# First feed-forward layer, second pass: six blocks of 512 tokens in place of eight of 384

## The chip, the cores and the metric

The kernel runs on one core of a Trainium2 chip. The metric is the device time of one execution in microseconds, median of several runs. The kernel before takes 2503.87 us (three runs, 2503.05 to 2504.59).

## What is computed

Three stages follow one another; `N` is 3072 tokens, the model width is 512.

```python
x = attention(q, k, v, mem_k, mem_v)        # chunks of 32 queries, 16 + 32 + 8 keys and 8 memory keys, 8 heads
h = x @ w_in                                # [3072, 512] @ [512, 2048]
g = h * np.clip(h + 3.0, 0.0, 6.0) / 6.0
x = g @ w_out                               # [2048, 512]: the "first layer" ends here
logits = x @ w_gate                         # 8 experts
P = exp(logits - logits.max())
for _ in range(8):                          # rows and columns in turn
    P /= P.sum(1, keepdims=True) + 1e-9
    P /= P.sum(0, keepdims=True) + 1e-9
    P *= N / 8
out = sum(P[:, e:e+1] * (np.maximum(x @ w1[e], 0) @ w2[e]) for e in range(8))
```

## The kernel before

Every large product is made of three matmuls in the float32r type: operands are split into a high and a low part, and `passes` (L224 to L228) issues high x high, high x low and low x high into the same accumulator. In the trace these are the lines L226, L227 and L228.

The first layer's inner width of 2048 is taken in two halves of 1024, the two **passes** `pe` = 0 and 1, each over all tokens in eight blocks `b` of `B1` = 384 tokens and, inside a block, over eight slices `f` of 128 inner columns. The list `steps` holds all (pe, b, f); the main loop near the end of the function walks it with the index `i`, 64 steps to a pass. A step of pass 1 issues

- `first(i)`: `layer_product` (12 matmuls into `ph`: four slices of the model width, three matmuls each), `layer_relu` on ACT (L399, tile `t`) and `layer_times` on DVE (L404);
- `first_parts(i)`: `layer_high` (L166 on DVE in pass 1, tile `hh`) and `layer_low` (L421 on DVE, tile `hl`);
- `second(i - LAG)` with `LAG` = 2: 12 matmuls into the four accumulators `pa` with the `hh` and `hl` of two steps earlier. At a block's last slice it calls `evacuate`: four DVE adds (L503) of `pa` to the `x2` of pass 0, which `x2_load` fetched from DRAM (`xp`, L483); the sums go back to DRAM as `x2d` in `spill` (L445).

Beside this, each block of pass 1 carries: `x_load(b + 1)` at f = 1 (the attention's result from DRAM, L509, tile `xl`, stored in units of `UQ` = 96 tokens), `x_split` at f = 3 to 6, one slice of the model width each (ACT L210 for `xh`, DVE L215 for `xl`), `x2_load(b)` at f = 4, and the gates of finished blocks: `gate_logits` (L524, four small matmuls per block, each shown as two rows), `gate_copy` (ACT, L529) and `gate_turn` (three transposes L537 and a DVE reduction L538). Gates are made at f = 3, two blocks together in blocks 2, 4 and 6 and one in block 7, the last one after the loop.

Two further jobs run under pass 1. `factory` makes 80 sums of the experts' weights: SP loads 512 KB (L640), POOL adds (L645), SP stores (L648); a table of start times in units of steps paces them. From step (1, 4, 0) `x_ops` prepares the first 1024 tokens for the experts, one piece per step: loads from `x2d` (L710, three buffers `xb`), DVE subtractions (L719), and splits into `xo` (L210 on ACT, L215 on DVE). In the last block the experts' first weights are loaded (`w1_load`, L787 and others) and copied and split (`w1_hi` on ACT, L806; `w1_lo` on DVE, L811), a piece per step from f = 1 on.

The order of instructions on each engine is the order in which the program issues them; DMAs are issued by SP, in order. The matmuls of the experts' stage that follows are 512 or 256 tokens wide.

Of the kernel before, what the change touches and what calls it, by code (L numbers as in the profile page):

```python
# [9 lines left out]
F32 = mybir.dt.float32  # L10
F32R = mybir.dt.float32r
# [9 lines left out]
UQ = 96  # L21
# [43 lines left out]
def attn_moe_moe(ctx: ExitStack, tc: tile.TileContext, qk, vw, wi, wo, wa, wb, wg, out):  # L65
# [5 lines left out]
    NTT = NT // 128  # L71
    NB1, NSB = NT // B1, NT // (2 * HB)
    UPB = B1 // UQ
# [25 lines left out]
    half = const.tile([128, 1], F32, name="half")  # L99
    wgs = const.tile([128, KT + 1, 32], F32, name="wgs")  # L100
    Pm = const.tile([128, NTT, NE], F32, name="Pm")
# [3 lines left out]
    xd = [dr_p.tile([128, B1 // UQ, KT, UQ], F32, name=f"xd{b}") for b in range(NB1)]  # L105
    xp = [dr_p.tile([128, KT, B1], F32, name=f"xp{b}") for b in range(NB1)]
    ws1 = [dr_p.tile([128, 4, 2, 256], F32, name=f"ws1{j}") for j in range(NP // 2)]
# [279 lines left out]
    g_t, acc_t, x2_t = {}, {}, {}  # L387

    def layer_product(i):
        pe, b, f = steps[i]  # L390
        wh, wl = (w.rearrange("p (k f) -> p k f", k=KT) for w in wts["a", pe, f])
        g_t[i] = ps = ps_h.tile([128, B1], F32, tag="h", name="ph")
        for kt in range(KT):
            hi, lo = (t[:, kt] for t in xs[pe, b])
            passes(ps, wh[:, kt], wl[:, kt], hi, lo, kt == 0, kt == KT - 1)

    def layer_relu(i):
        t = h_p.tile([128, B1], F32, tag="t", name="t", bufs=2)
        nc.scalar.activation(out=t, in_=g_t[i], func=AF.Relu, scale=1.0 / 6.0, bias=half)  # L399
        g_t[i] = g_t[i], t  # L400
# [11 lines left out]
    def layer_high(i, eng=nc.scalar):  # L412
        t = g_t[i]
        hh = h_p.tile([128, B1], F32R, tag="hh", name="hh")
        copy(hh, t, nc.vector if steps[i][0] else eng)
        g_t[i] = t, hh

    def layer_low(i):
        t, hh = g_t[i]
        hl = h_p.tile([128, B1], F32R, tag="hl", name="hl")  # L420
        nc.vector.tensor_tensor(out=hl, in0=t, in1=hh.bitcast(F32), op=ALU.subtract)  # L421
        g_t[i] = hh, hl
# [5 lines left out]
    def second(i, out=True):  # L428
        pe, b, f = steps[i]
        turns = (0, NF // 2) if (pe, b) in ((0, 0), (0, 1)) else (0,)  # L430
        new, last = f in turns, f + 1 in turns or f == NF - 1
        if new:
            acc_t[pe, b] = [ps_a.tile([128, 512], F32, tag="a", name="pa")[:, :B1] for _ in range(4)]
# [47 lines left out]
    def x2_load(b):  # L481
        t = x2_t[b] = x2_p.tile([128, KT, B1], F32, tag="x2", name="x2")
        nc.sync.dma_start(out=t, in_=xp[b])  # L483

    def evacuate(pe, b, f):
        acc = acc_t.pop((pe, b))
        if pe == 0 and b in x2_t:
            x2 = x2_t.pop(b)
            for t in range(4):
                nc.vector.tensor_tensor(out=x2[:, t], in0=x2[:, t], in1=acc[t], op=ALU.add)  # L490
            spills.append((xp[b], x2))
        elif pe == 0:
            x2 = x2_p.tile([128, KT, B1], F32, tag="x2", name="x2")
            for t in range(4):
                nc.scalar.activation(out=x2[:, t], in_=acc[t], func=AF.Copy)
            if f < NF - 1:
                x2_t[b] = x2
            else:
                spills.append((xp[b], x2))
        else:  # L500
            x2 = x2_t[b]
            for t in range(4):
                nc.vector.tensor_tensor(out=x2[:, t], in0=x2[:, t], in1=acc[t], op=ALU.add)  # L503
            spills.append((x2d[:, :, b * B1:(b + 1) * B1], x2))
            later.append(b)

    def x_load(b):
        t = xf_t[b] = xl_p.tile([128, UPB, KT, UQ], F32, tag="xl", name="xl")
        nc.sync.dma_start(out=t, in_=xd[b])  # L509

    def x_split(b, kt):
        if kt == 0:
            xs[1, b] = x_tiles()
        hi, lo = (t[:, kt].rearrange("p (u q) -> p u q", u=UPB) for t in xs[1, b])
        split(hi, lo, xf_t[b][:, :, kt])

# [4 lines left out]
    def gate_logits(b):  # L521
        ps = ps_s.tile([128, B1], F32, tag="s", name="lg")
        for kt in range(KT):
            nc.tensor.matmul(ps[32 * kt:32 * kt + 32], wgs[:, kt], x2_t[b][:, kt], start=True, stop=True)  # L524
        lg[b] = ps

    def gate_copy(b):
        ps, lg[b] = lg[b], sm_p.tile([128, B1], F32, tag="lt", name="lt", bufs=1)
        nc.scalar.activation(out=lg[b], in_=ps, func=AF.Copy)  # L529

    def gate_turn(b):
        if b < NB1 - 1:
            ps = ps_s.tile([128, B1 // 128, 128], F32, tag="s", name="lg")
        else:
            ps = bank().rearrange("p (t k) -> p t k", k=128)[:, :B1 // 128]
        for i in range(B1 // 128):
            nc.tensor.transpose(ps[:, i], lg[b][:, 128 * i:128 * i + 128], ident)  # L537
        nc.vector.tensor_reduce(  # L538
            out=Pm[:, 3 * b:3 * b + 3], in_=ps.rearrange("p t (k e) -> p t e k", k=KT)[:, :, :NE],
            axis=AX.X, op=ALU.add)  # L540

    def sinkhorn():
# [13 lines left out]
        for _ in range(8):  # L556
            rs = sm_p.tile([128, NTT], F32, tag="rs", name="rs")
            nc.vector.tensor_reduce(out=rs, in_=Pm, axis=AX.X, op=ALU.add)
# [125 lines left out]

    def x_quarters(form, r0, r1, eng=nc.vector):

        l, h = slice(0, 256), slice(256, 512)
        quarter_tile(form)
        quarter_parts(form, ("B11",), r0[:, l])
# [13 lines left out]
    def x_ops(sb, p, tag):  # L703
# [3 lines left out]
        def load(n, kt, half_):  # L707
            xq[n] = p.tile([128, 2, HB], F32, tag=tag, name="xb", bufs=3)
# [6 lines left out]
        for n in X_ORDER:  # L715
# [11 lines left out]
            yield  # L727
        yield from x_quarters("B21", xq["B21"][:, 0], xq["B21"][:, 1])

# [351 lines left out]
    with tc.manual_schedule():  # L1081
# [17 lines left out]
        starts = [15 + 1.27 * j for j in range(len(jobs))]  # L1099
        xb_ctx = ctx.enter_context(ExitStack())  # L1100
        for i, (pe, b, f) in enumerate(steps):
            if i < 2 * NF:
# [9 lines left out]
            if (pe, b, f) == (1, NB1 - 1, 0):  # L1112
                assert build is None and begun[2] == len(jobs)
# [13 lines left out]
            for stage_, late in ((2, 2.6), (0, 0), (1, 1.3)):  # L1127
                while begun[stage_] < len(jobs) and starts[begun[stage_]] + late <= i:
                    jobs[begun[stage_]][stage_]()
                    begun[stage_] += 1  # L1130
# [4 lines left out]
            if pe == 1 and f == 1 and b + 1 < NB1:  # L1135
# [5 lines left out]
            if ready and f == 4:  # L1141
                gate_copy(later[0])
            first(i)
            if pe or due:
                first_parts(i)
            if due:
# [30 lines left out]
            r = f - 3  # L1177
            if 0 <= r < KT and n < NB1 and (pe or b == NB1 - 1):
# [231 lines left out]
```

## Time and profile before

| | |
|---|---|
| runs, median (lowest to highest) | 2503.87 us (2503.05 to 2504.59) |
| the profiled execution's own time | 2502.63 us |
| its span | 2500.8 us |
| PE busy | 2488.2 us, 99% of the span |
| DVE busy | 1971.4 us, 79% |
| ACT busy | 1444.4 us, 58% |
| POOL busy | 955.4 us, 38% |
| TensorE clock granted | 9 tenths or more in each of 40 slices |
| DMA | 586.72 MB, mean 235 GB/s |

The span goes from the first to the last instruction of the profiled execution; its own time is 1.8 us more. Starts of matmuls are recorded, their ends are modelled, so the spacing of matmuls is read from their starts. Pass 1 of the first layer lies between 378 and 657 us of the span.

### The profile page before, as it was taken

What the parts mean: (1) busy time and instruction counts of PE and PEld (TensorE: products, weight loads), DVE (VectorE), ACT (ScalarE), POOL (GpSimd) and SP (SyncE); (2) the same over time, 40 slices, a digit from 0 to 9 for tenths busy, and PEclk for the clock granted to TensorE, in tenths of its full rate; (3) what the DMA queues carried; (4) which work ended last, traced back from release to release, by engine and by line L of the source; (5) the groups of instructions that cost most, each with busy time, mean ns of one, the idle gap of its engine ahead of it and who ended that gap; (6) DMA issues with size and microseconds to landing.
All of it is one profiled execution on the core that took longest, in us unless ns stands there. A gap on an engine that the chain in (4) does not pass through costs nothing. (4 is left out here: it accounts for less than half of the span.)

```text
span 2500.8 us, 37810 instructions
## 1 busy us (share of the span) xinstructions
PE 2488.2 (99%) x13525; PEld 2172.8 (87%) x13525; DVE 1971.4 (79%) x2432; ACT 1444.4 (58%) x2647; POOL 955.4 (38%) x705
## 2 busy tenths in 40 slices
PE   9999999999999999999999999999999999999999
PEld 8999999999878888888888888888888888888888
DVE  8767656576689999999996778777887678777777
ACT  8666652222365555556666656556666666655665
POOL 0155656564026453544443324333333233232331
PEclk9999999999999999999999999999999999999999
DMA  7689979877466667766667777666777666676664
GB/s 209 190 277 310 305 267 312 268 272 244 129 210 207 225 208 233 232 228 218 233 223 264 266 249 247 223 217 231 251 266 233 226 221 231 225 235 208 215 220 157
DMA packets 373754, 586.72 MB, mean 235 GB/s; under 512 B 30324, under 2 KB 227133, under 8 KB 373565
## 3 DMA queue, kind: packets, MB, share of 16 engines
q1 hardware_dynamic: 373280, 584.06, 71.7%
q8 instruction: 106, 1.74, 0.3%
q14 instruction: 84, 0.68, 0.1%
q10 hardware_dynamic: 284, 0.24, 0.0%
HBM read 443.57 MB, written 140.61 MB: 234 GB/s over the span
## 5 line engine op out<-in xcount | busy, mean ns | idle before, releaser
L933 POOL TENSOR_TENSOR g<-g,pb 128x512 f32<-128x512 f32 x304 | 578.4, 1920 | 1175.6 <-ACT g L926 830.4
L984 ACT ACTIVATE oh<-g 128x1024 fp32r<-128x1024 f32 x336 | 355.1, 1057 | 356.9 <-PE oa L228 107.1
L989 DVE TENSOR_TENSOR ol<-g,oh 128x1024 fp32r<-128x1024 f32 x336 | 458.5, 1366 | 54.0 <-ACT oh L984 53.8
L645 POOL TENSOR_TENSOR fr<-fr 128x256 f32<-128x256 f32 x320 | 268.6, 840 | 191.4 <-DMA fr<-in_wa_dram 109.2
L226 PE MATMUL ga<-xo,w1h 128*128 128x512 f32 (+1 forms) x864 | 313.8, 363 | 1.4 <-ACT g L901 0.8
L228 PE MATMUL ga<-xo,w1l 128*128 128x512 f32 (+1 forms) x864 | 312.2, 361 | 0.0
L227 PE MATMUL ga<-xo,w1h 128*128 128x512 f32 (+1 forms) x864 | 312.2, 361 | 0.0
L959 DVE TENSOR_TENSOR g<-g 128x1024 f32<-128x1024 f32 x192 | 306.0, 1632 | 0.0
L227 PE MATMUL oa<-ol,w2h 128*128 128x512 f32 x760 | 297.9, 392 | 0.4 <-DVE ol L989 0.4
L226 PE MATMUL oa<-oh,w2h 128*128 128x512 f32 x760 | 297.3, 391 | 0.0
L228 PE MATMUL oa<-oh,w2l 128*128 128x512 f32 x760 | 295.7, 389 | 0.0
L806 ACT ACTIVATE w1h<-w1s 128x512 fp32r<-128x512 f32 (+1 forms) x416 | 249.7, 600 | 35.3 <-issue 16.0
L399 ACT ACTIVATE t<-ph,half 128x384 f32<-128x384 f32 x128 | 74.8, 584 | 242.2 <-PE ph L228 235.9
L918 DVE TENSOR_TENSOR g<-g,ga 128x512 f32<-128x512 f32 x192 | 130.5, 680 | 103.4 <-PE ga L228 103.4
L926 ACT ACTIVATE g<-g 128x512 f32<-128x512 f32 x288 | 178.2, 619 | 53.4 <-DVE g L918 53.1
L226 PE MATMUL gc<-xo,w1h 128*128 128x512 f32 (+1 forms) x544 | 195.4, 359 | 2.3 <-ACT g L901 1.8
L228 PE MATMUL gc<-xo,w1l 128*128 128x512 f32 (+1 forms) x544 | 194.5, 357 | 0.0
L227 PE MATMUL gc<-xo,w1h 128*128 128x512 f32 (+1 forms) x544 | 194.4, 357 | 0.0
L843 ACT ACTIVATE w2h<-w2s 128x1024 fp32r<-128x1024 f32 x168 | 176.8, 1052 | 27.5 <-DMA w2s<-in_wb_dram 21.7
L226 PEld LDWEIGHTS ga<-xo,w1h 128*128 128x128 f32 x864 | 162.5, 188 | 34.6 <-ACT g L901 2.4
L227 PEld LDWEIGHTS ga<-xo,w1h 128*128 128x128 f32 x864 | 162.5, 188 | 28.6
L228 PEld LDWEIGHTS ga<-xo,w1l 128*128 128x128 f32 x864 | 162.4, 188 | 25.2
(184 smaller groups left out, 5779.1 us busy)
## 6 DMA issues: line engine op xcount, KB each, us to landing
w1l<-wl SPq DMA_DIRECT2D x232, 256.0 KB, 4.2
w2l<-wl SPq DMA_DIRECT2D x112, 512.0 KB, 3.7
w1s<-ws SPq DMA_DIRECT2D x192, 256.0 KB, 4.9
w2s<-ws SPq DMA_DIRECT2D x96, 512.0 KB, 5.0
ws<-fr SPq DMA_DIRECT2D x80, 512.0 KB, 5.0
w2s<-in_wb_dram SPq DMA_DIRECT2D x144, 256.0 KB, 3.6
wl<-w1l SPq DMA_DIRECT2D x128, 256.0 KB, 4.2
wl<-w2l SPq DMA_DIRECT2D x56, 512.0 KB, 4.2
```

Of the source, the lines that this page charges most:

```text
L226: nc.tensor.matmul(ps, wh, xh, start=start, stop=False, skip_group_check=more)
L227: nc.tensor.matmul(ps, wh, xl, start=False, stop=False, skip_group_check=more)
L228: nc.tensor.matmul(ps, wl, xh, start=False, stop=stop, skip_group_check=more)
L645: nc.gpsimd.tensor_tensor(out=o, in0=a, in1=b, op=f)
L806: nc.scalar.activation(out=w1_part(g, w1[g]), in_=w1_part(g, w1s[g]), func=AF.Copy)
L843: nc.scalar.activation(out=hi, in_=w2s[m], func=AF.Copy)
L918: nc.vector.tensor_tensor(out=g, in0=g, in1=ps, op=ALU.add)
L926: nc.scalar.activation(out=g, in_=g, func=AF.Relu)
L933: nc.gpsimd.tensor_tensor(out=g, in0=g, in1=p, op=ALU.mult)
L959: nc.vector.tensor_tensor(out=o, in0=gq[n, x, i], in1=gq[n, y, i], op=ALU.subtract)
L984: nc.scalar.activation(out=hi, in_=gq[n, b, i], func=AF.Copy)
L989: nc.vector.tensor_tensor(out=lo, in0=gq[n, b, i], in1=op[m, i].bitcast(F32), op=ALU.subtract)
```

## The change

Pass 1 (the second pass) takes tokens in `NB2` = 6 blocks of `B2` = 512, so it has 48 steps instead of 64; pass 0 keeps its 64 steps of 384. What goes with it:

- The split x of pass 1 no longer takes a new pair of tiles per block. Three pairs of the old tiles are taken once and seen as pieces [128, 3, 512]: even blocks use pair 0 and one piece of pair 1, odd blocks pair 2 and another piece of pair 1. The third piece of pair 1 holds two units of 96 tokens of the x that is loaded, since the one `xl` tile holds four units and a block touches up to six.
- A block of 512 does not begin on a unit of 96, so `x_load` issues three or four transfers, and `x_split` makes three or four pieces per slice of the model width.
- `x2` of a block fills both buffers of its pool, half of the model width in each: two loads, two spills. The pass-0 result lies in one DRAM tensor `xpd`.
- The gates of each block are made at f = 3 of the next, all in one step, 512 tokens at a time (four transposes).
- The paced jobs count a step of pass 1 as `PACE` = 1.308 steps and are also looked at half-way through a step.
- `x_ops` starts at step (1, 2, 6), with two `xb` buffers; a third piece lies in the `xo` tile that is filled last. The experts' first weights begin two slices later in the last block (f = 2 for the loads, f = 3 to 6 for the copies).

```diff
-    steps = [(pe, b, f) for pe in range(2) for b in range(NB1) for f in range(NF)]
+    steps = [(pe, b, f) for pe in range(2) for b in range((NB1, NB2)[pe]) for f in range(NF)]
...
         for kt in range(KT):
-            hi, lo = (t[:, kt] for t in xs[pe, b])
+            hi, lo = (t[:, kt] for t in xs[pe, b]) if pe == 0 else xs[pe, b][kt]
             passes(ps, wh[:, kt], wl[:, kt], hi, lo, kt == 0, kt == KT - 1)
...
     def x2_load(b):
-        t = x2_t[b] = x2_p.tile([128, KT, B1], F32, tag="x2", name="x2")
-        nc.sync.dma_start(out=t, in_=xp[b])
+        x2_t[b] = []
+        for j in range(2):
+            t = x2_p.tile([128, KT, B1], F32, tag="x2", name="x2").rearrange("p k n -> p (k n)")
+            t = t[:, :2 * B2].rearrange("p (k n) -> p k n", k=2)
+            nc.sync.dma_start(out=t, in_=xpd[:, 2 * j:2 * j + 2, b * B2:(b + 1) * B2])
+            x2_t[b].append(t)
...
     def x_load(b):
-        t = xf_t[b] = xl_p.tile([128, UPB, KT, UQ], F32, tag="xl", name="xl")
-        nc.sync.dma_start(out=t, in_=xd[b])
+        if b < 2:
+            xq.extend(x_pieces() for _ in range(2 - b))
+        for kt in range(KT):
+            n, at = ((0, kt) if kt < 3 else (1, 0)) if b % 2 == 0 else ((2, kt) if kt < 3 else (1, 1))
+            xs.setdefault((1, b), []).append([t[:, at] for t in xq[n]])
+        u = b * B2 // UQ
+        t = xl_p.tile([128, UPB, KT, UQ], F32, tag="xl", name="xl")
+        spare = [v[:, 2, :KT * UQ].bitcast(F32).rearrange("p (k q) -> p k q", k=KT) for v in xq[1]]
+        c = UPB - u % UPB
+        nc.sync.dma_start(out=t[:, :c], in_=xd[u // UPB][:, UPB - c:])
+        if c < UPB:
+            nc.sync.dma_start(out=t[:, c:], in_=xd[u // UPB + 1][:, :UPB - c])
+        for i in range(2):
+            v = u + UPB + i
+            nc.sync.dma_start(out=spare[i], in_=xd[v // UPB][:, v % UPB])
...
     def gate_turn(b):
-        if b < NB1 - 1:
-            ps = ps_s.tile([128, B1 // 128, 128], F32, tag="s", name="lg")
+        if b < NB2 - 1:
+            ps = ps_s.tile([128, B2 // 128, 128], F32, tag="s", name="lg")
...
+        def sums_due(i):
+            now = i if i <= NB1 * NF else NB1 * NF + (i - NB1 * NF) * PACE
+            for stage_, late in ((2, 2.6), (0, 0), (1, 1.3)):
+                while begun[stage_] < len(jobs) and starts[begun[stage_]] + late <= now:
+                    jobs[begun[stage_]][stage_]()
+                    begun[stage_] += 1
...
-            if (pe, b) == (1, NB1 - 1) and 1 <= f <= AHEAD:
-                w1_hi(f - 1)
-                w1_lo(f - 1)
-                if f < AHEAD:
-                    w1_load(f + 3)
+            if (pe, b) == (1, NB2 - 1) and 3 <= f <= AHEAD + 2:
+                w1_hi(f - 3)
+                w1_lo(f - 3)
+                if f < AHEAD + 2:
+                    w1_load(f + 1)
...
-            if pe == 1 and f == 4:
+            if pe == 1 and f == 5:
                 x2_load(b)
-            ready = pe == 1 and (f == 3 and len(later) > (b < NB1 - 1) or f == 4 and later and later[0] in lg)
+            ready = pe == 1 and f == 3 and later
...
-            if (pe, b, f) == (1, 4, 0):
+            if (pe, b, f) == (1, 2, 6):
                 build = x_ops(0, xb_p, "xb")
```

Where instructions move, engine by engine. On DVE in the last block of the first pass, where the first x of the second pass is split (`wal`, `wbl`: low parts of the layer's weights; `xl`: low part of x), before:

```order
L404 SCALAR_TENSOR_TENSOR t<-t,ph 128x384
L421 TENSOR_TENSOR hl<-t,hh 128x384
L215 TENSOR_TENSOR wal<-sa,wah 128x512
L215 TENSOR_TENSOR wbl<-sb,wbh 128x512
L215 TENSOR_TENSOR xl<-xl,xh 128x384
```

and with the change:

```order
L410 SCALAR_TENSOR_TENSOR t<-t,ph 128x384
L427 TENSOR_TENSOR hl<-t,hh 128x384
L218 TENSOR_TENSOR wal<-sa,wah 128x512
L218 TENSOR_TENSOR wbl<-sb,wbh 128x512
L218 TENSOR_TENSOR xl<-xl,xh 128x384
L218 TENSOR_TENSOR xl<-xh 128x96
L218 TENSOR_TENSOR xl<-xl,xh 128x32
```

The split of one slice has become three pieces (four in later blocks), each behind a piece of the same shape on ACT.

On PE at a block's f = 3 in the middle of the second pass, between the layer's product `ph` and the second product `pa`, before:

```order
L227 MATMUL ph<-xl,wah 128x384
L228 MATMUL ph<-xh,wal 128x384
L524 MATMUL lg<-x_6193,wgs 32x384 x4
L524 MATMUL lg<-x_6521,wgs 32x384 x4
L226 MATMUL pa<-hh,wbh 128x384
L227 MATMUL pa<-hl,wbh 128x384
```

and with the change:

```order
L230 MATMUL ph<-xl,wah 128x512
L231 MATMUL ph<-xh,wal 128x512
L571 MATMUL lg<-x_6357,wgs 32x512 x2
L571 MATMUL lg<-x_6359,wgs 32x512 x2
L229 MATMUL pa<-hh,wbh 128x512
L230 MATMUL pa<-hl,wbh 128x512
```

Two blocks' logits, eight matmuls, have become one block's four, from two half tiles.

On SP's queue in the middle of the second pass, from the load of x to the spill of the block before (`ws<-fr` and `fr<-in` are the paced sums), before:

```order
L509 DMA xl<-xd_121 128x1536
L648 DMA ws_145<-fr 512x1x256
L640 DMA fr<-in_wb_dram 128x1024
L445 DMA x2d<-x_6521 512x1x384
L648 DMA ws_154<-fr 512x1x256
```

and with the change:

```order
L533 DMA xl<-xd_121 128x1152
L535 DMA xl<-xd_122 128x384
L538 DMA xh<-xd_122 128x384
L538 DMA xl<-xd_122 128x384
L695 DMA ws_138<-fr 512x1x256
L687 DMA fr<-in_wb_dram 128x1024
L451 DMA x2d<-x_6357 128x2x512
L451 DMA x2d<-x_6359 128x2x512
L695 DMA ws_147<-fr 512x1x256
```

Where two transfers of the layer stood among the sums' own, six stand now.

## Rows read from the trace of the kernel before

**Rows 1.** Busy time by stretch: us; each engine's busy us (instructions); clock, DMA share, GB/s.

```profile
377.99:656.86 278.87, 278.87 (x1638) 273.81 (x1637) 177.78 (x287) 67.53 (x124) 146.10 (x175) 1.00 0.75 250
541.00:556.00 15.00, 15.00 (x88) 15.00 (x87) 13.38 (x16) 4.62 (x7) 10.50 (x10) 1.00 0.48 145
```

**Rows 2.** Timeline of PE, second pass: start us, us, engine, line, operation, out<-in, shapes.

```profile
377.99 0.33 PE L226 MATMUL ph<-xh,wah 128*128 128x384 f32 x1
...
457.03 0.33 PE L226 MATMUL ph<-xh,wah 128*128 128x384 f32 x1
...
656.69 0.34 PE L228 MATMUL pa<-hh,wbl 128*128 128x384 f32 x1
```

**Rows 3.** Timeline of PE, experts' stage: matmuls 256 and 512 tokens wide.

```profile
659.02 0.28 PE L227 MATMUL ga<-xo,w1h 128*128 128x256 f32 x1
...
659.38 0.28 PE L227 MATMUL gb<-xo,w1h 128*128 128x256 f32 x1
...
1175.83 0.40 PE L226 MATMUL oc<-oh,w2h 128*128 128x512 f32 x1
...
1236.83 0.39 PE L228 MATMUL oa<-oh,w2l 128*128 128x512 f32 x1
```

**Rows 4.** Timeline of PE, gates of two blocks and of one block.

```profile
459.20 1.50 PE L524 MATMUL lg<-x,wgs 128*32 128x384 f32 x16
460.63 0.44 PE L226 MATMUL pa<-hh,wbh 128*128 128x384 f32 x1
...
632.43 0.34 PE L228 MATMUL ph<-xh,wal 128*128 128x384 f32 x1
632.70 0.85 PE L524 MATMUL lg<-x,wgs 128*32 128x384 f32 x8
633.49 0.45 PE L226 MATMUL pa<-hh,wbh 128*128 128x384 f32 x1
...
635.71 0.49 PE L537 MATMUL lg<-ident,lt 128*128 128x128 f32 x3
635.95 0.42 PE L226 MATMUL ph<-xh,wah 128*128 128x384 f32 x1
...
636.56 0.34 PE L226 MATMUL ph<-xh,wah 128*128 128x384 f32 x1
```

**Rows 5.** Timeline of all engines, end of the second pass.

```profile
655.51 2.12 DVE L503 TENSOR_TENSOR x<-x,pa 128x384 f32<-128x384 f32 x4 [2.45 <-PE pa L228]
...
658.44 0.39 PE L226 MATMUL ga<-xo,w1h 128*128 128x256 f32 x1
```

**Rows 6.** Groups by line, shapes apart, 378 to 657 us: count | busy us, mean ns | idle before.

```profile
L421 DVE TENSOR_TENSOR hl<-t,hh 128x384 fp32r<-128x384 f32 x65 | 50.5, 776 | 2.8 <-ACT hh L164 0.6
L399 ACT ACTIVATE t<-ph,half 128x384 f32<-128x384 f32 x64 | 37.3, 583 | 194.7 <-PE ph L228 194.7
L404 DVE SCALAR_TENSOR_TENSOR t<-t,ph 128x384 f32<-128x384 f32 x64 | 35.3, 552 | 83.8 <-ACT t L399 83.7
L166 DVE CAST hh<-t 128x384 fp32r<-128x384 f32 x64 | 28.5, 445 | 5.4
L215 DVE TENSOR_TENSOR xl<-xl,xh 128x384 fp32r<-128x384 f32 x28 | 22.8, 813 | 0.0
...
L503 DVE TENSOR_TENSOR x<-x,pa 128x384 f32<-128x384 f32 x31 | 15.2, 545 | 2.5 <-PE pa L228 2.5
...
L215 DVE TENSOR_TENSOR xo<-xb,xo 128x1024 fp32r<-128x1024 f32 x6 | 8.7, 1455 | 0.0
```

**Rows 7.** Groups by line, shapes apart, whole span: an add from PSUM, 512 wide.

```profile
L1018 DVE TENSOR_TENSOR y<-y,oa 128x512 f32<-128x512 f32 x172 | 117.0, 680 | 38.3 <-PE oa L228 38.1
```

**Rows 8.** The tile xl, 340 to 660 us: its DMA issues, ns min/median/max.

```profile
L509 SPq DMA_DIRECT2D xl<-xd x8: 430/838/1248, 352.0 to 589.2; - x8
```

**Rows 9.** Timelines of SP and ACT: the experts' first weights.

```profile
610.40 1.29 SPq L787 DMA_DIRECT2D w1s<-in_wa_dram  x2
...
620.81 0.62 ACT L806 ACTIVATE w1h<-w1s 128x512 fp32r<-128x512 f32 x1
```

More of the change, by code (lines that the diff above doesn't have):

```diff
@@ L33 @@
 HB = 512
+B2 = 512
+PACE = 1.308
 NEG = -2.0 ** 100
@@ L71, in attn_moe_moe @@
     NTT = NT // 128
-    NB1, NSB = NT // B1, NT // (2 * HB)
+    NB1, NB2, NSB = NT // B1, NT // B2, NT // (2 * HB)
     UPB = B1 // UQ
@@ L99, in attn_moe_moe @@
     half = const.tile([128, 1], F32, name="half")
-    wgs = const.tile([128, KT + 1, 32], F32, name="wgs")
+    wgs = const.tile([128, KT, 32], F32, name="wgs")
     Pm = const.tile([128, NTT, NE], F32, name="Pm")
@@ L105, in attn_moe_moe @@
     xd = [dr_p.tile([128, B1 // UQ, KT, UQ], F32, name=f"xd{b}") for b in range(NB1)]
-    xp = [dr_p.tile([128, KT, B1], F32, name=f"xp{b}") for b in range(NB1)]
+    xpd = dr_p.tile([128, KT, NT], F32, name="xpd")
+    xp = [xpd[:, :, b * B1:(b + 1) * B1] for b in range(NB1)]
     ws1 = [dr_p.tile([128, 4, 2, 256], F32, name=f"ws1{j}") for j in range(NP // 2)]
@@ L380, in attn_moe_moe, with width @@
     xf_t = {}
-    steps = [(pe, b, f) for pe in range(2) for b in range(NB1) for f in range(NF)]
+    steps = [(pe, b, f) for pe in range(2) for b in range((NB1, NB2)[pe]) for f in range(NF)]
     steps[:2 * NF] = [(0, b, f + g) for g in (0, NF // 2) for b in range(2) for f in range(NF // 2)]
     g_t, acc_t, x2_t = {}, {}, {}
+    def width(i):
+        return (B1, B2)[steps[i][0]]
     def layer_product(i):
@@ L391, in layer_product @@
         wh, wl = (w.rearrange("p (k f) -> p k f", k=KT) for w in wts["a", pe, f])
-        g_t[i] = ps = ps_h.tile([128, B1], F32, tag="h", name="ph")
+        g_t[i] = ps = ps_h.tile([128, 512], F32, tag="h", name="ph")[:, :width(i)]
         for kt in range(KT):
-            hi, lo = (t[:, kt] for t in xs[pe, b])
+            hi, lo = (t[:, kt] for t in xs[pe, b]) if pe == 0 else xs[pe, b][kt]
             passes(ps, wh[:, kt], wl[:, kt], hi, lo, kt == 0, kt == KT - 1)
     def layer_relu(i):
-        t = h_p.tile([128, B1], F32, tag="t", name="t", bufs=2)
+        t = h_p.tile([128, 512], F32, tag="t", name="t", bufs=2)[:, :width(i)]
         nc.scalar.activation(out=t, in_=g_t[i], func=AF.Relu, scale=1.0 / 6.0, bias=half)
@@ L413, in layer_high @@
         t = g_t[i]
-        hh = h_p.tile([128, B1], F32R, tag="hh", name="hh")
+        hh = h_p.tile([128, 512], F32R, tag="hh", name="hh")[:, :width(i)]
         copy(hh, t, nc.vector if steps[i][0] else eng)
@@ L419, in layer_low @@
         t, hh = g_t[i]
-        hl = h_p.tile([128, B1], F32R, tag="hl", name="hl")
+        hl = h_p.tile([128, 512], F32R, tag="hl", name="hl")[:, :width(i)]
         nc.vector.tensor_tensor(out=hl, in0=t, in1=hh.bitcast(F32), op=ALU.subtract)
@@ L432, in second @@
         if new:
-            acc_t[pe, b] = [ps_a.tile([128, 512], F32, tag="a", name="pa")[:, :B1] for _ in range(4)]
+            acc_t[pe, b] = [ps_a.tile([128, 512], F32, tag="a", name="pa")[:, :width(i)] for _ in range(4)]
         acc = acc_t[pe, b]
@@ L500, in evacuate @@
         else:
-            x2 = x2_t[b]
             for t in range(4):
-                nc.vector.tensor_tensor(out=x2[:, t], in0=x2[:, t], in1=acc[t], op=ALU.add)
-            spills.append((x2d[:, :, b * B1:(b + 1) * B1], x2))
+                x2 = x2_t[b][t // 2][:, t % 2]
+                nc.vector.tensor_tensor(out=x2, in0=x2, in1=acc[t], op=ALU.add)
+                if t % 2:
+                    spills.append((x2d[:, t - 1:t + 1, b * B2:(b + 1) * B2], x2_t[b][t // 2]))
             later.append(b)
+    xq = []
@@ L507, in x_load, with x_pieces @@
+    def x_pieces():
+        return [t.rearrange("p k n -> p (k n)").rearrange("p (k n) -> p k n", n=B2) for t in x_tiles()]
     def x_load(b):
-        t = xf_t[b] = xl_p.tile([128, UPB, KT, UQ], F32, tag="xl", name="xl")
-        nc.sync.dma_start(out=t, in_=xd[b])
-    def x_split(b, kt):
[L512 to L515, printed above, removed]
+        if b < 2:
[13 more added lines that the diff above has]
+            nc.sync.dma_start(out=spare[i], in_=xd[v // UPB][:, v % UPB])
+        parts = []
+        for i in range(UPB + 2):
+            a, e = (min(max(v - b * B2, 0), B2) for v in (UQ * (u + i), UQ * (u + i + 1)))
+            o = a + b * B2 - UQ * (u + i)
+            whole = i < UPB and e - a == UQ
+            if whole and parts and parts[-1][0] == "whole":
+                parts[-1] = "whole", parts[-1][1], e, parts[-1][3], i + 1
+            elif whole:
+                parts.append(("whole", a, e, i, i + 1))
+            else:
+                parts.append(("part", a, e, t[:, i] if i < UPB else spare[i - UPB], o))
+        xf_t[b] = t, parts
@@ L518, in attn_moe_moe @@
+    def x_split(b, kt):
+        hi, lo = xs[1, b][kt]
+        t, parts = xf_t[b]
+        for kind, a, e, v, o in parts:
+            if kind == "whole":
+                src = t[:, v:o, kt]
+                to = [w[:, a:e].rearrange("p (u q) -> p u q", q=UQ) for w in (hi, lo)]
+            else:
+                src = v[:, kt, o:o + e - a]
+                to = [w[:, a:e] for w in (hi, lo)]
+            split(*to, src)
     lg = {}
@@ L521, in gate_logits @@
     def gate_logits(b):
-        ps = ps_s.tile([128, B1], F32, tag="s", name="lg")
+        ps = ps_s.tile([128, B2], F32, tag="s", name="lg")
         for kt in range(KT):
-            nc.tensor.matmul(ps[32 * kt:32 * kt + 32], wgs[:, kt], x2_t[b][:, kt], start=True, stop=True)
+            nc.tensor.matmul(ps[32 * kt:32 * kt + 32], wgs[:, kt], x2_t[b][kt // 2][:, kt % 2], start=True, stop=True)
         lg[b] = ps
     def gate_copy(b):
-        ps, lg[b] = lg[b], sm_p.tile([128, B1], F32, tag="lt", name="lt", bufs=1)
+        ps, lg[b] = lg[b], sm_p.tile([128, B2], F32, tag="lt", name="lt", bufs=1)
         nc.scalar.activation(out=lg[b], in_=ps, func=AF.Copy)
     def gate_turn(b):
-        if b < NB1 - 1:
-            ps = ps_s.tile([128, B1 // 128, 128], F32, tag="s", name="lg")
-        else:
-            ps = bank().rearrange("p (t k) -> p t k", k=128)[:, :B1 // 128]
-        for i in range(B1 // 128):
+        if b < NB2 - 1:
+            ps = ps_s.tile([128, B2 // 128, 128], F32, tag="s", name="lg")
+        else:
+            ps = bank().rearrange("p (t k) -> p t k", k=128)
+        for i in range(B2 // 128):
             nc.tensor.transpose(ps[:, i], lg[b][:, 128 * i:128 * i + 128], ident)
         nc.vector.tensor_reduce(
-            out=Pm[:, 3 * b:3 * b + 3], in_=ps.rearrange("p t (k e) -> p t e k", k=KT)[:, :, :NE],
+            out=Pm[:, 4 * b:4 * b + 4], in_=ps.rearrange("p t (k e) -> p t e k", k=KT)[:, :, :NE],
             axis=AX.X, op=ALU.add)
@@ L556, in sinkhorn @@
         for _ in range(8):
-            rs = sm_p.tile([128, NTT], F32, tag="rs", name="rs")
+            rs = sm_p.tile([128, B2], F32, tag="lt", name="rs", bufs=1)[:, :NTT]
             nc.vector.tensor_reduce(out=rs, in_=Pm, axis=AX.X, op=ALU.add)
@@ L683, in quarter_sum, with x_quarters @@
         eng.tensor_tensor(out=to, in0=a, in1=b, op=ALU.subtract)
-    def x_quarters(form, r0, r1, eng=nc.vector):
+    def x_quarters(form, r0, r1, eng=nc.vector, new=True):
         l, h = slice(0, 256), slice(256, 512)
-        quarter_tile(form)
+        if new:
+            quarter_tile(form)
         quarter_parts(form, ("B11",), r0[:, l])
@@ L707, in load @@
         def load(n, kt, half_):
-            xq[n] = p.tile([128, 2, HB], F32, tag=tag, name="xb", bufs=3)
+            if n == "B22":
+                quarter_tile("B21")
+                xq[n] = xo["B21"][:, 0].bitcast(F32).rearrange("p a t -> p (a t)")[:, :2 * HB]
+                xq[n] = xq[n].rearrange("p (k t) -> p k t", k=2)
+            else:
+                xq[n] = p.tile([128, 2, HB], F32, tag=tag, name="xb", bufs=2)
             at = (2 * sb + half_) * HB
@@ L727, in x_ops @@
             yield
-        yield from x_quarters("B21", xq["B21"][:, 0], xq["B21"][:, 1])
+        yield from x_quarters("B21", xq["B21"][:, 0], xq["B21"][:, 1], new=False)
     def x_source(sb, n, q):
@@ L1111, in attn_moe_moe @@
                 xb_p = xb_ctx.enter_context(pool("xb", 1, side="right"))
-            if (pe, b, f) == (1, NB1 - 1, 0):
+            if (pe, b, f) == (1, NB2 - 1, 2):
                 assert build is None and begun[2] == len(jobs)
@@ L1120, in attn_moe_moe @@
                 w2_load(0)
-            if (pe, b) == (1, NB1 - 1) and 1 <= f <= AHEAD:
-                w1_hi(f - 1)
-                w1_lo(f - 1)
-                if f < AHEAD:
-                    w1_load(f + 3)
[L1127 to L1130, printed above, removed]
+            if (pe, b) == (1, NB2 - 1) and 3 <= f <= AHEAD + 2:
[3 more added lines that the diff above has]
+                    w1_load(f + 1)
+            sums_due(i)
             if pe == 0 and b == NB1 - 1:
@@ L1134, in attn_moe_moe @@
                     x_load(0)
-            if pe == 1 and f == 1 and b + 1 < NB1:
+            if pe == 1 and f == 1 and b + 1 < NB2:
                 x_load(b + 1)
-            if pe == 1 and f == 4:
+            if pe == 1 and f == 5:
                 x2_load(b)
-            ready = pe == 1 and (f == 3 and len(later) > (b < NB1 - 1) or f == 4 and later and later[0] in lg)
+            ready = pe == 1 and f == 3 and later
             spill()
-            if ready and f == 4:
-                gate_copy(later[0])
             first(i)
@@ L1152, in attn_moe_moe @@
                 stage(v_load, u + 2)
-            if ready and f == 3:
-                for n in later:
-                    gate_logits(n)
+            if ready:
+                gate_logits(later[0])
                 gate_copy(later[0])
@@ L1159, in attn_moe_moe @@
                 gate_turn(later.pop(0))
+            if pe:
+                sums_due(i + 0.5)
             if due:
@@ L1177, in attn_moe_moe @@
             r = f - 3
-            if 0 <= r < KT and n < NB1 and (pe or b == NB1 - 1):
+            if 0 <= r < KT and n < NB2 and (pe or b == NB1 - 1):
                 x_split(n, r)
-            if (pe, b, f) == (1, 4, 0):
+            if (pe, b, f) == (1, 2, 6):
                 build = x_ops(0, xb_p, "xb")
```

## The prediction

> **What bounds the kernel now.** I read the busy time by stretch first, for the stretch that the change rewrites [rows 1]: from the first matmul of the second pass to its last, 278.87 us, PE is busy for all 278.87 us, at a granted clock of 1.00 (the 2.4 GHz level). DVE is busy for 177.78, POOL for 146.10, ACT for 67.53. A busy PE alone proves little, since ends of matmuls are modelled, so the second view is PE's timeline, where only starts count. The 456 matmuls from 377.99 to 457.03 [rows 2] start 79.04 / 456 = 0.17333 us apart, without one exception. So in this stretch each matmul removed shortens the kernel and nothing else does, unless another engine becomes late.
>
> What a matmul costs beyond its columns is seen by comparing widths. 384 columns at 2.4 GHz take 160.0 ns, so 13.3 ns are left over. 256-wide matmuls: three starts in 0.36 us [rows 3], 120.0 ns, of which 106.7 are columns: 13.3. 512-wide ones: 269 intervals in 61.00 us [rows 3], 226.77 ns, of which 213.33 are columns: 13.4. Three widths, one fixed part per instruction.
>
> **Part 1, the matmuls: -5.0 us.** A step is 24 matmuls, whatever its width. Before: 64 steps x 24 x 0.17333 = 266.24 us. After: 48 x 24 x 0.22677 = 261.23 us. Columns are the same, 384 matmuls fewer, 5.01 us less. Were the fixed part exactly 13.33 ns, it would be 5.12.
>
> The Trainium skill ("TensorE: Matmul & The Clock Gate", section "Back-to-back issue gap") gives the warm spacing as columns / 2.4 + 2.5 ns. By that the 384 matmuls would save 0.96 us and not 5.0; the three widths above contradict it here, so the sum goes by the rows.
>
> **Part 2, the gates: +0.2 us.** These small matmuls do interrupt the even spacing [rows 4]. A single block's gates (logits and three transposes) lie between the starts at 632.43 and 636.56, 4.13 us, in which 16 ordinary spacings (2.77) also lie: 1.36 us. Two blocks together take 1.43 us from the first logit to the next product, one block 0.79: eight more matmul rows cost 0.64 us, and these go with columns. All of it in the second pass: from 377.99 to 656.69 + 0.17 it has 1,560 ordinary matmuls [rows 2], 270.40 us, leaving 8.47 us for three pairs and one single. After, there are five singles of 512 columns. Each costs 1.36 + 0.64 x 1/3 (0.21) + one more transpose (0.24 / 3 = 0.08) = 1.65, together 8.25: -0.22. The last block's gates stand open at the end: from the last product's start to the experts' first, 656.69 to 658.44 [rows 2, 5]. PE there waits for the last of four DVE adds, 545 ns at 384 [rows 6] against 680 at 512 [rows 7]: +0.13, columns +0.21, the fourth transpose +0.08, together +0.42. Sum of the part +0.20.
>
> **Part 3, DVE and ACT: nothing, with cover.** The chain from a finished `ph` to `hl` is relu, times, cast, low: 583 + 552 + 445 + 776 ns [rows 6], 2.4 us, and some 3.0 at 512. `second` comes three half-steps after the product, before 3 x 2.08, after 3 x 2.72 = 8.16 us: 5 us of slack. The densest steps are those that also split x and build the experts' input; there DVE is busy for 13.38 of 15 us [rows 1]. Per step now: 552 + 445 + 776 + 813 + 1455 [rows 6] = 4.04 of 4.16 us. For 512 columns I take the slope of the add, (680 - 545) / 128 = 1.05 ns a column and 0.14 us fixed: times 0.69, cast 0.58, low and the 512 columns of x by 4/3 as upper ends (1.03 and 1.08), three more pieces of x 0.42, the build's piece as it is: 5.26 of 5.44 us. If every piece costs twice its fixed part, 5.7, so DVE would fall behind by 0.3 us in each of some eight such steps, 2.4 us, still inside the 5.
>
> At a block's end `pa` must be copied out in time: four adds of 0.68 behind `hl`. The first ends 3.0 + 0.7 us after the product `ph` of that step, and PE wants its accumulator 5.44 us after it: 1.7 us of slack, as now (2.4 + 0.55 against 4.16, 1.2). The first x of the pass is split in pass 0's last block, into three pieces instead of one; two more pieces on ACT and DVE per step lie under PE there too. If this cover goes, the price is the delay beyond the slack, once per block end. A gain beyond the removed matmuls is excluded, since no wait of PE is left to remove in the stretch.
>
> **Part 4, SP and POOL: nothing, with cover.** The layer's transfers grow from 8 x 3 to 22 + 12 + 12 = 46; SP's issue of an `xl` takes 0.84 us (0.43 to 1.25) [rows 8], so 22 x 0.84 = 18.5 us more in SP's queue, in 274 us. Behind them wait the sums' loads and stores, hence POOL, and behind the sums the experts' first weights. These are asked for at 610.40 and first used at 620.81 [rows 9], behind a relu and not behind their DMA: at most 10.4 us were needed. After, that use stands ahead of the relu of step (1, 5, 3), due at about 620. POOL has 132.8 us to spare in the stretch, so I count nothing; the upper end is rival C.
>
> **Sum.** -5.01 + 0.20 = -4.8 us. The profiled execution took 2502.63 us (span 2500.8), 1.2 below the median of the runs, and becomes 2497.8; against the median, 2503.87 - 4.8 = **2499.1 us**. About 0.2%, or 5.0 us, is what a measurement of this kernel can tell from no change: the forecast lies on that line, 0.19% faster. Its own range is 2497.8 to 2500.3: 5.1 to 4.3 us of gain, with the 0.8 us by which the three runs lie about their median.
>
> **Rivals.**
>
> A. *The fixed part does not go with the instruction in this stretch.* The 512-wide rows are of the experts' stage; with the layer's operands the spacing might grow by 4/3, to 231.1 ns, and 1,152 of them are as long as 1,536 now: 2503.87 + 0.20 = 2504.1. For it: no row of the layer at 512. Against it: 256 and 512 in the other stage and 384 in this one give the same 13.3 to 13.4. The skill's 2.5 ns, above, is a milder form of it; by it the time would be 2503.1. Chance 0.04.
>
> B. *DVE falls behind* in the steps that both split and build, or where the pass begins: PE waits once or twice at `pa` or at the last slice of x. Decides when the delay passes the 1.7 us at a block's end. Price 2 us, for a block's four adds late by 1 us in each of the two blocks under the build: 2501.1. For it: 5.26 to 5.7 us of DVE work in 5.44. Against: it is 97% now as well, and no wait of PE shows. Chance 0.09.
>
> C. *SP's queue runs late and the experts' first weights with it.* If none of the 18.5 us is covered, they are asked for at 628.9; with 10.4 us to come, ACT stands before the relu of step (1, 5, 3) until 639.3 instead of 620. Less the 5 us of slack, PE loses 14 us: 2499.1 + 14 = 2513, slower than before. Decides once the request is more than 5 us later than 610.4. For it: SP is in order, and stores wait in it for POOL. Against: POOL and DMA (share 0.75 [rows 1]) have room, so SP's waits shrink as its work grows. Chance 0.05.
>
> **How the numbers follow.** Forecast 0.82, A 0.04, B 0.09, C 0.05. The forecast lies on the line of 0.2%; its uncertain 0.4 us and the scatter of the runs split it 0.43 faster and 0.39 same. A and B are same, C slower: faster 0.43, same 0.52, slower 0.05. The range of 8 in 10 takes in the forecast's own range and B: 2497.8 to 2502.0.
>
> **What would show it.** Right: starts of `ph` and `pa` 0.2268 us apart in the second pass; from its first matmul to its last 261.2 + 4.2 (two products of pass 0) + 8.2 = 273.6 us, after 278.9; no row under PE's waits there; 1.9 to 2.2 us in place of 1.75 at the end; the experts' stage as long as before. Wrong: 231 ns (A); waits of `pa` or `ph` for DVE near block ends (B); `w1s` requested after 615 and ACT idle before `w1h` on a DMA (C). A changed experts' stage would mean a cause that this sum does not hold.

## The result and the profile after

The changed kernel takes 2518.31 us (median of 6 runs, 2517.79 to 2519.08), the kernel before 2502.99 in the same session (6 runs, 2502.86 to 2504.59): a ratio of 1.0060, 95% interval 1.0047 to 1.0073. It is 15.3 us slower; the forecast was 2499.1, in a range of 2497.8 to 2502.0, with a chance of 0.05 for slower.

The page of the changed kernel, engines' busy time and the slices of the granted clock:

```profile
PE 2502.8 (99%) x13125; PEld 2119.0 (84%) x13125; DVE 1970.4 (78%) x2430; ACT 1444.7 (57%) x2685; POOL 924.8 (37%) x705
...
PEclk9999999999999999999999999999999999999999
```

PE is busy for 14.6 us more than before, at an unchanged clock. To see where, two stretches of the span are read: from the first matmul of the second pass to one spacing behind the start of its last product, and from the first matmul of the experts' stage to the end. Busy time by stretch, changed kernel (columns as in [rows 1]):

```profile
378.20:652.13 273.93, 273.93 (x1237) 222.66 (x1236) 173.23 (x281) 66.84 (x154) 147.63 (x176) 1.00 0.75 254
...
654.04:2516.50 1862.46, 1854.30 (x8930) 1544.62 (x8929) 1524.54 (x1673) 1124.85 (x1680) 615.56 (x344) 1.00 0.68 225
```

and the second of these stretches in the kernel before:

```profile
658.44:2500.80 1842.36, 1833.83 (x8929) 1546.29 (x8928) 1522.32 (x1673) 1124.41 (x1680) 650.04 (x344) 1.00 0.69 227
```

The second pass, which the change rewrites, takes 273.93 us instead of the 278.87 of [rows 1]. The experts' stage, which it does not touch, takes 1862.46 instead of 1842.36, 20.1 us more, with the same numbers of instructions on PE, DVE, ACT and POOL (one record more or less), the same clock and a DMA share of 0.68 against 0.69. PE is idle there for 8.2 us, before for 8.5. With 0.2 us more ahead of the second pass and 0.3 us more between the two stretches, the span adds up: 0.2 - 4.9 + 0.3 + 20.1 = 15.7 us, from 2500.8 to 2516.5. The extra time lies inside PE's busy time, so only starts can show it. The timeline of PE in the changed kernel, the first and last matmul of the run of 512-wide ones that [rows 3] shows of before:

```profile
1177.23 0.40 PE L229 MATMUL oc<-oh,w2h 128*128 128x512 f32 x1
...
1239.24 0.39 PE L231 MATMUL oa<-oh,w2l 128*128 128x512 f32 x1
```

These are the same 269 intervals: 61.00 us before, 62.01 now, 226.77 ns against 230.52 for one. The stage holds 7,080 such matmuls; 20.1 us over them is 2.8 ns each on average (3.75 in this run). PE waits no longer than before: the stage's matmuls themselves start further apart.

What differs, then, for instructions that are the same? Their addresses. Three edits of the change, which the prediction did not mention, alter the size of small tiles that are placed before the layer's and the experts' buffers on the left side of SBUF:

```diff
-    wgs = const.tile([128, KT + 1, 32], F32, name="wgs")
+    wgs = const.tile([128, KT, 32], F32, name="wgs")
...
-        ps, lg[b] = lg[b], sm_p.tile([128, B1], F32, tag="lt", name="lt", bufs=1)
+        ps, lg[b] = lg[b], sm_p.tile([128, B2], F32, tag="lt", name="lt", bufs=1)
...
-            rs = sm_p.tile([128, NTT], F32, tag="rs", name="rs")
+            rs = sm_p.tile([128, B2], F32, tag="lt", name="rs", bufs=1)[:, :NTT]
```

Per partition that is 128 bytes less, 512 more and 2 x 96 less: the experts' buffers on the left start 192 bytes higher. So do the layer's, or higher by 192 and a multiple of 256, since its tiles `t`, `hh` and `hl` became 512 bytes longer each. The placement of the built programs says so (first byte in each partition; the last column is the remainder by 256):

```
                       before             after
w2h  (left)         5856  (224)        6048  (160)
oh   (left)        79584  (224)       79776  (160)
w1h  (right)      141280  (224)      141280  (224)
xo   (right)      165856  (224) ...  165856  (224) ...
```

In the kernel before every operand of the experts' matmuls has the remainder 224. In the changed one the left ones (`w2h`, `w2l`, `oh`, `ol`) have 160, the right ones (`w1h`, `w1l`, `xo`) 224. The seven `xo` tiles also stand in another order, since the largest is now touched first.

### The profile page after: what moved, and what is told of

Same layout as the page of the kernel before. It is cut to its first block, busy times and chain, and to the rows that moved or that the text cites. A ratio compares the mean times of both kernels' runs of the same rounds, so it can differ in the third digit from the quotient of the medians.

```text
span 2516.5 us, 37071 instructions
## 1 busy us (share of the span) xinstructions
PE 2502.8 (99%) x13125; PEld 2119.0 (84%) x13125; DVE 1970.4 (78%) x2430; ACT 1444.7 (57%) x2685; POOL 924.8 (37%) x705
## 5 line engine op out<-in xcount | busy, mean ns | idle before, releaser
L986 POOL TENSOR_TENSOR g<-g,pb 128x512 f32<-128x512 f32 x304 | 542.8, 1802 | 1221.8 <-ACT g L979 871.4
L405 ACT ACTIVATE t<-ph,half 128x384 f32<-128x384 f32 (+1 forms) x112 | 70.5, 629 | 241.5 <-PE ph L231 235.2
```

What stands on the lines that cost most here:

```text
L986: nc.gpsimd.tensor_tensor(out=g, in0=g, in1=p, op=ALU.mult)
```

## The experiments

**First four: which side.** One kernel moves only the left buffers of the changed kernel, by 64 bytes more; one moves only the left buffers of the kernel before, by the 192; the other two exchange the order of `xo` between the kernels. No instruction differs otherwise.

```diff
+        sm_p.tile([128, 16], F32, tag="pad", name="pad", bufs=1)
         for _ in range(8):
...
                 xo_p = ctx.enter_context(pool("xo", 1, side="right"))
+                quarter_tile("B21")
```

The pad is that of e1, in the changed kernel; in e2, in the kernel before, it is [128, 48]. The line on `quarter_tile` is e3, in the kernel before; e4 takes the six other `xo` tiles first in the changed kernel. In e2 the experts' left buffers stand exactly where the changed kernel has them; of the layer's, those behind `t` have only the same remainder by 256.

> The changed kernel with 64 unused bytes per partition behind the small tiles, so that every buffer opened on the left of SBUF after them (the experts' w2h, w2l, oh, ol, g, y, pb and the layers' weights) starts 256 bytes above its place in the kernel before instead of 192; nothing else moves. Theory LEFT (the 512-wide matmuls of the experts' stage became 3 to 5 ns slower because the left buffers moved by 192 bytes): about 2498 us, 20 us under the changed kernel's 2518. Theory XO (they became slower because the xo tiles stand in another order on the right): 2518, as without the pad. Theory BOTH (the 2,672 matmuls on w2h by the left shift, some 10 us, the 2,048 that read xo's high part by the order of xo, some 10 us): about 2508. Theory TIMING (no address matters; other engines' work falls differently): 2518.

> The kernel before with 192 unused bytes per partition at the same place, so that its left buffers of the layers and of the experts stand exactly where the changed kernel has them; instructions are the same. LEFT: about 2523 us, 20 over the kernel before. XO: 2503. BOTH: about 2513. TIMING: 2503.

> The kernel before with the 14,336-byte xo tile placed first instead of last, so that all seven xo tiles stand where the changed kernel has them; left buffers and instructions are the same. LEFT: 2503 us. XO: about 2523. BOTH: about 2513. TIMING: 2503.

> The changed kernel with its seven xo tiles placed in the order of the kernel before; left buffers (192 bytes higher) and instructions are as changed. LEFT: 2518 us. XO: about 2498. BOTH: about 2508. TIMING: 2518.

| kernel | us, median (runs) | ratio to before, 95% interval |
|---|---|---|
| e1, changed, left 64 higher | 2498.74 (10) | 0.9984 (0.9974 to 0.9994) |
| e2, before, left 192 higher | 2522.70 (4) | 1.0081 (1.0066 to 1.0096) |
| e3, before, xo as changed | 2502.56 (10) | 0.9999 (0.9990 to 1.0008) |
| e4, changed, xo as before | 2518.17 (4) | 1.0062 (1.0047 to 1.0077) |

LEFT gave all four numbers; XO, BOTH and TIMING fell. A kernel with the old second pass and only the new places loses 20.0 us, the kernel with the new second pass and 64 bytes of padding is 4.0 us faster than before (its interval runs from 1.5 to 6.5). The timeline of PE shows it on the same 269 intervals, in the padded changed kernel (e1), 61.00 us:

```profile
1171.87 0.40 PE L229 MATMUL oc<-oh,w2h 128*128 128x512 f32 x1
...
1232.87 0.39 PE L231 MATMUL oa<-oh,w2l 128*128 128x512 f32 x1
```

and in the kernel before with its left buffers moved (e2), 62.01 us:

```profile
1181.94 0.40 PE L226 MATMUL oc<-oh,w2h 128*128 128x512 f32 x1
...
1243.95 0.39 PE L228 MATMUL oa<-oh,w2l 128*128 128x512 f32 x1
```

LEFT does not say why, and one thing speaks against its simplest form: the second pass has all its operands on the left, moved to the same new remainder, and was not slowed. Two starts from the timeline of the changed kernel, 178 intervals of 512-wide matmuls in it, 40.36 us, 226.74 ns each:

```profile
444.28 0.39 PE L230 MATMUL ph<-xl,wah 128*128 128x512 f32 x1
...
484.64 0.39 PE L231 MATMUL ph<-xh,wal 128*128 128x512 f32 x1
```

So either other engines' work takes part (it is denser in the experts' stage), or what counts is not where the left buffers stand but how they stand to the right ones: the experts' stage alternates six matmuls on `xo` and `w1` with six on `oh`, `ol` and `w2`.

**Next three: place or relation.** e5 moves the left buffers of the kernel before up by 192 and all right ones down by 64; e6 only the right ones; e7 only the left ones, by 128.

```diff
     const = ctx.enter_context(pool("const", 1))
+    ctx.enter_context(pool("rpad", 1, side="right")).tile([128, 16], F32, tag="rpad", name="rpad")
...
+        sm_p.tile([128, 48], F32, tag="pad", name="pad", bufs=1)
```

e5 has both lines, e6 the first, e7 the second with [128, 32].

> The kernel before with its left buffers 192 bytes higher (as in the second run, which took 2522.7 us) and all its right buffers 64 bytes lower (an unused 64-byte tile opened first on the right), so that both sides move to the same place modulo 256. Theory RELATION (a matmul stream slows when operands that follow each other start at different places modulo 256; the experts' stage mixes triples on right buffers, xo with w1, and on left buffers, oh and ol with w2): about 2503 us, since left and right agree again. Theory PLACE (what counts is where the left buffers themselves stand): 2522.

> The kernel before with only its right buffers 64 bytes lower; left buffers as in the kernel before, instructions the same. RELATION: about 2522 us, some 20 slower, though no left buffer moved. PLACE: 2503.

> The kernel before with its left buffers 128 bytes higher, so that left and right agree modulo 128 but not modulo 256. RELATION with a period of 128 bytes or less: 2503 us. RELATION with a period of 256: some 10 to 20 us slower. PLACE says nothing on this size.

| kernel | us, median (runs) | ratio to before, 95% interval |
|---|---|---|
| e5, left +192, right -64 | 2502.60 (10) | 0.9998 (0.9989 to 1.0007) |
| e6, right -64 | 2522.91 (4) | 1.0080 (1.0063 to 1.0096) |
| e7, left +128 | 2514.63 (4) | 1.0048 (1.0033 to 1.0063) |

RELATION holds and PLACE falls: the right side alone costs the same 20 us, and moving both sides costs nothing. Agreement modulo 128 is not enough; the price at 128 is smaller, 11.8 us. In the timeline of PE the same intervals take 62.01 us in e6,

```profile
1181.16 0.39 PE L227 MATMUL oc<-oh,w2h 128*128 128x512 f32 x1
...
1243.17 0.39 PE L229 MATMUL oa<-oh,w2l 128*128 128x512 f32 x1
```

and 61.44 us in e7, 228.40 ns each:

```profile
1178.49 0.39 PE L226 MATMUL oc<-oh,w2h 128*128 128x512 f32 x1
...
1239.93 0.40 PE L228 MATMUL oa<-oh,w2l 128*128 128x512 f32 x1
```

**The period, by itself.** e8 is the kernel before with 256 bytes on the left (a pad of [128, 64]).

> The kernel before with its left buffers 256 bytes higher; everything else as before. RELATION with a period of 256 bytes: 2503 us, no change (and then the 2498.7 us of the first run, whose left buffers stand at the same place, comes from the changed second pass and not from this place). If the period is longer: 10 to 20 us slower. If this place is better in itself: under 2503.

It took 2503.16 us (11 runs), ratio 1.0000 (0.9991 to 1.0009). With a price at 64, 128 and 192 bytes and none at 256, the period is 256 bytes, and the gain of e1 is not that of its place but of the second pass.

**A bench without other engines.** The first bench replaces the whole computation by streams of matmuls. `triple(t, a, b)` stands for three matmuls with weights and moving operands from tile `t`, moved by a and b bytes.

```diff
+    for d in [32 * v for v in range(16)]:
+        plans.append(("g", d, (triple(rr, 0, 0) * 2 + triple(ll, d, d) * 2) * 10))
...
+        plans.append(("a", d, triple(rr, d, d) * 40))
```

> None of the reference's work is done: 56 streams of 120 matmuls (128x512, float32r, a weight load each, no other engine at work) read two resident tiles, ll on the left and rr on the right, both starting at 224 modulo 256. Streams pg: two triples on rr, two on ll, the ll ones moved up by d = 0 to 480 bytes in steps of 32 (letters a to p); pc: the same with both halves in rr; ps: weights alone moved by d against the moving operand; pa: all moved by d together; pm: every second moving operand moved; pw: every second weight tile moved. RELATION: pg and pc take 227 ns a matmul at d = 0 and 256 and some 230 ns or more at the d that stand for the shifts of 64 and 192; pa stays at 227 at each d. PLACE: pa itself changes with d, and pg as pa does. CONTENTION (the spacing grows only where other engines write to SBUF at the same time): all streams stay at 227 at each d.

The timeline of PE, where each stream begins (`pgc` to `pge` have d = 64 to 128, `pgi` has 256, `paa` to `pac` move all operands by 0, 32 and 64; in `pmg` and `pmh` every second moving operand is moved, by 192 and 224):

```profile
72.34 1.53 PE L112 MATMUL pgc<-rr 128*128 128x512 f32 x6
...
100.00 1.55 PE L112 MATMUL pgd<-rr 128*128 128x512 f32 x6
...
127.73 1.55 PE L112 MATMUL pge<-rr 128*128 128x512 f32 x6
...
155.53 1.55 PE L112 MATMUL pgf<-rr 128*128 128x512 f32 x6
...
238.53 1.54 PE L112 MATMUL pgi<-rr 128*128 128x512 f32 x6
...
265.75 1.53 PE L112 MATMUL pgj<-rr 128*128 128x512 f32 x6
...
682.20 27.37 PE L112 MATMUL paa<-rr 128*128 128x512 f32 x120
...
736.64 27.40 PE L112 MATMUL pac<-rr 128*128 128x512 f32 x120
...
1066.01 27.38 PE L112 MATMUL pmg<-rr 128*128 128x512 f32 x120
1093.23 27.77 PE L112 MATMUL pmh<-rr 128*128 128x512 f32 x120
```

A stream has 120 matmuls, so the difference of two starts by 120 is one matmul: `pgc` 230.5 ns, `pge` 27.80 / 120 = 231.7, `pgi` 27.22 / 120 = 226.8, `paa` and `pab` together 54.44 / 240 = 226.8. CONTENTION falls: nothing but PE runs here, and the spacing still grows. PLACE falls again: moved together, the operands cost nothing.

The other streams, read in the same way: `pc`, with both halves in `rr`, gives the numbers of `pg` within 0.1 ns at every d from 32 to 224, so that the two sides of SBUF play no part. The second half of `pg`, d = 256 to 480, repeats the first. With one weight tile and every second moving operand moved (`pm`), a matmul takes 230.1 to 233.3 ns at every d but 0 and 192; with one moving operand and every second weight tile moved (`pw`), 229.9 to 234.9 at every d but 0. One stream goes against RELATION as it is worded: `pmg`, with d = 192, takes 27.22 / 120 = 226.8 ns and pays nothing. Equal remainders are enough, then, but in that one layout they are not needed.

Sizes did not carry over from this bench to the kernels (231.7 here at 128, 228.4 in e7), so a second bench replays the stage's own addresses, 480 matmuls of it in their order, with all else idle.

```diff
+    for i in range(9):
+        for k, (w, x) in enumerate(SEQ):
+            nc.tensor.matmul(t, op(w, 128, 32 * i), op(x, 512, 32 * i), start=k == 0, stop=k == len(SEQ) - 1)
```

> None of the reference's work is done: 480 consecutive 512-wide matmuls of the experts' stage of the kernel before are replayed from two resident tiles with their own operand addresses (modulo 1024, and in their distances), nine times, the left operands moved up by d = 0, 32, ... 256 bytes (qa to qi), with every other engine idle. In the kernels themselves a 512-wide matmul of that stage takes 227.5 ns at d = 0, 229.1 at 128 and 230.6 at 192. If the sizes come from the operands' addresses alone: qa and qi 227, qe (128) about 229 and qg (192) about 230.5. If they follow the first bench, whose operands are laid out otherwise: qe 231.7, qc and qg 230.5. If other engines' work takes part in them: some other value, and none of the kernels'.

The timeline of PE, first and last group of six on the right side in the streams for d = 128 (`qe`), 192 (`qg`) and 256 (`qi`); 432 matmuls lie between:

```profile
460.93 1.55 PE L180 MATMUL qe<-rr 128*128 128x512 f32 x6
...
559.54 1.53 PE L180 MATMUL qe<-rr 128*128 128x512 f32 x6
...
681.10 1.54 PE L180 MATMUL qg<-rr 128*128 128x512 f32 x6
...
780.52 1.54 PE L180 MATMUL qg<-rr 128*128 128x512 f32 x6
...
901.62 1.53 PE L180 MATMUL qi<-rr 128*128 128x512 f32 x6
...
999.55 1.52 PE L180 MATMUL qi<-rr 128*128 128x512 f32 x6
```

228.3, 230.1 and 226.7 ns. The kernels show 228.4 at 128 (e7), 230.5 at 192 (the changed kernel, e2) and 226.8 at 0 and 256. The whole curve of both benches, ns a matmul, worked out in the same way:

| d, bytes | 0 | 32 | 64 | 96 | 128 | 160 | 192 | 224 | 256 |
|---|---|---|---|---|---|---|---|---|---|
| first bench, `pg` (`pca` at 0, since `pga` holds the start of the run) | 226.7 | 229.9 | 230.5 | 231.1 | 231.7 | 231.1 | 230.6 | 230.0 | 226.8 |
| replay | 226.7 | 229.8 | 230.2 | 230.7 | 228.3 | 230.7 | 230.1 | 229.7 | 226.7 |

So the addresses alone give the kernels' sizes to within 0.4 ns of a price of up to 3.75; no other engine is needed. The kernels' numbers here are those of the 269 intervals, which alternate in sixes throughout as the replay does; the 227.5, 229.1 and 230.6 of the expectation are means over the whole stage, up to 0.8 ns higher than the replay. (The replay's stream for d = 0 also holds the start of the run; its value is from later groups, 2.72 us for 12 matmuls.)

The kept traces also show where in a group of six the price is paid, as the mean time from a matmul's start to the next one's, over the 460 to 490 groups of each side that a group of the other side follows. At 128 bytes (e7) it is paid at the change of side alone: 232.5 ns from the last matmul of a group to the next group, 231 from the first matmul to the second, and 226.8 to 227.1 at the four others. At 192 (e2) it is spread over the group, 228.4, 229.6, 233.0, 235.2, 224.6 and 231.1 ns on the right side, and the replay has the same pattern there: 228.3, 229.2, 233.4, 235.8, 224.2 and 231.7.

## Why the prediction was wrong

The step that failed is one line of its list of what would show it right: "the experts' stage as long as before". The sum counted the stretch that the change rewrites and put the rest at nothing without a reason. What the runs showed in its place: the stage became 20.1 us longer, and e2 charges 20.0 us to the places of the left buffers alone, with the instructions of before; e5 and e6 show that it is their place against the right ones that counts. The text did say that a changed experts' stage would need a cause outside its sum, but gave it no chance and no price.

Its own terms held:

- **Matmuls (-5.0 us): right.** 226.74 ns in the second pass against the 226.77 used; rival A (231.1) fell. The stretch was forecast at 273.6 us and took 273.93. The Trainium skill's rule ("TensorE: Matmul & The Clock Gate", "Back-to-back issue gap") of 2.5 ns beyond the columns, which that section gives for an isolated matmul, does not fit here either: 226.74 - 213.33 = 13.4 ns.
- **Gates (+0.2): near.** Without 1,152 products (261.2) and two of pass 0 (4.2), 8.5 us are left for five gates, forecast 8.25. At the end, from the last product's start to the experts' first matmul, 2.14 us, forecast 1.75 + 0.42 = 2.17; the timeline of PE in the changed kernel:

```profile
651.90 0.39 PE L231 MATMUL pa<-hh,wbl 128*128 128x512 f32 x1
652.22 1.90 PE L571 MATMUL lg<-x,wgs 128*32 128x512 f32 x8
654.04 0.39 PE L229 MATMUL ga<-xo,w1h 128*128 128x256 f32 x1
```

- **DVE and ACT at nothing: right.** No wait of PE lies in the stretch. Groups by line there, against the estimates of at most 1.03 us for the low part (L427), 0.69 for times (L410) and 0.58 for the cast (L169); rival B, DVE late, fell:

```profile
L427 DVE TENSOR_TENSOR hl<-t,hh 128x512 fp32r<-128x512 f32 x48 | 42.8, 892 | 1.7
L410 DVE SCALAR_TENSOR_TENSOR t<-t,ph 128x512 f32<-128x512 f32 x48 | 33.0, 687 | 83.1 <-ACT t L405 82.8
L169 DVE CAST hh<-t 128x512 fp32r<-128x512 f32 x48 | 27.6, 575 | 4.0
```

- **SP at nothing: right.** The experts' first weights are asked for at 610.52 us, before at 610.40 [rows 9], and first used at 616.15; ACT waits 0.19 us for them, PE not at all (rival C fell). Timelines of SP and ACT in the changed kernel:

```profile
610.52 1.32 SPq L840 DMA_DIRECT2D w1s<-in_wa_dram  x2
...
616.15 0.63 ACT L859 ACTIVATE w1h<-w1s 128x512 fp32r<-128x512 f32 x1 [0.19 <-DMA w1s<-ws]
```

One figure of its range was added up wrongly: 2503.87 - 5.1 - 0.8 is 2498.0, not 2497.8.

With 64 bytes of padding the kernel takes 2498.74 us, 0.4 below the forecast, and is 4.0 faster than before in the same session where 4.8 was forecast. That is the version to keep: it beats both kernels.

## What to carry to other kernels

When a change alters the size of any tile, compare the places of all tiles that are opened after it, not only the instructions: the sizes of a few small tiles (here `wgs`, `lt` and `rs`) may be what holds operands of distant stages in step. Where a stream of 512-wide float32r matmuls, the only kind tested here, alternates between buffers, give their starts the same remainder by 256 bytes; here 64 bytes of padding are worth 19.6 us, 0.8% of the kernel. When a stage that nobody touched changes, and its waits and its clock do not, measure start to start of the same instructions in both traces before looking for a new wait.

## What the runs showed of the hardware

In a steady stream a 512-wide float32r matmul with its own weight load takes 226.7 ns start to start when operands that follow each other start at the same place modulo 256 bytes, wherever that place is (the `pa` streams: 226.7 to 227.0 ns at each of eight places). Where the stream alternates in sixes between two places it takes up to 231.7, with a period of 256 bytes. In the first bench, moving only the weights against the moving operand costs 228.9 to 234.3 ns a matmul (`ps`, every d but 0). Beside matmuls of another width the spacing wanders even at equal remainders: in the padded kernel (e1), where the second pass begins among 384-wide matmuls of the first, some starts lie 233 to 236 ns apart.

How the size comes about stays open. Matmuls inside a group of six, whose neighbours share their remainder, pay at 192 bytes and not at 128, and `pmg` pays nothing at 192. The curve of the first bench is highest at 128 bytes, the replay has a dip there, and the two differ in the distances between their operands, which were not varied by themselves. Nor was it followed up that POOL's 304 operations on `g` took 1802 ns each in the changed kernel and 1920 before; with 1866 in e5 (2502.6 us) and 1880 in e4 (2518.2 us), they do not go with the kernel's time.
